# A prepared weight pair that stays on chip, resident loads spread over the steps, and an even credit table for late weight work

## The chip, the core and the metric

One core of a Trainium2 chip runs the whole kernel. The metric is device time in microseconds, as the median of repeated executions; lower is better. The engines are named by short names: PE (TensorE, matrix products), DVE (VectorE), ACT (ScalarE), POOL (GpSimd) and SP (SyncE, which only issues transfers). ACT issues transfers too.

## What is computed

Attention with two softmaxes (queries over the head dimension, keys over the sequence), then two MLPs, all in fp32:

```python
kv  = einsum('bhsd,bhde', softmax(k, seq), v)
x   = softmax(q, head_dim) @ kv          # 8 batches x 576 tokens, 512 wide
h   = x @ w_in1;  g = h * sigmoid(h);           x = g @ w_out1
h   = x @ w_in2;  g = h * clip(h + 3, 0, 6)/6;  out = g @ w_out2
```

There are 4608 tokens, and each MLP goes 512 to 2048 to 512.

## The kernel before

The tokens are cut into 9 blocks of 512 (`NB`), the 2048 hidden columns into 8 pairs of 128-column groups (`NC`); the program calls a pair p. One pair of one block is a cycle g of the first MLP (72 cycles, `PER`) or a step k of the second.

A product with w_in is done on 2 x 2 blocks with seven products instead of eight (Winograd's form), and each fp32 factor is split into a high and a low part, with three matmuls for each product (`mm3`, L76 to L79). So a pair of w_in has to be *prepared*: the raw words are turned into floats, sums of quarters are formed, and seven quarter-size forms are split into high and low. A prepared pair takes 14 KB per partition, 1792 KB in all. `converting` and `operands_w` write this as a list of (cost, function) items: magnitude (ACT), floor, shift, sign, low (DVE), two pairs of sums (DVE), then for two parts of three and four forms a cast on ACT (`high`, L207) and the remainder on DVE (`low`, L211), and a store of each part to DRAM (`keep_part`, L217, issued on ACT).

**First MLP.** `cycle(g)` does the seven w_in products of pair p (into the PSUM banks A, B and C, with the sums L771, L776 and L781 on DVE between them), the gate (`bend`), and between the products the eight w_out products of the cycle before (`layer_out`). The prepared w_in pair for cycle g + 2 is loaded from DRAM into a ring of two tiles (`load_w`). After each group of matmuls comes a `side(k)`, k from 0 to 7. There, from cycle 57 on (`LATE` is 56), the preparation of the second MLP's eight w_in pairs is worked off: `pump(more)` adds `more` to a credit and runs the items whose cost the credit covers. The items of all pairs stand in one list, made by `chain`, which puts the first item of a pair, the load of the next raw weights (`feed`, L101, on ACT) and the last store of the pair before next to one another.

**Second MLP, first half.** `step_in(k, slot)` does the seven products of a step, overlapped with its neighbours. Its prepared pairs stay on chip: pairs 0 and 1 in the ring's two tiles, 2 and 3 in tiles loaded in the last cycle (`keep_in(2, 4, 4)`), 4 to 7 in tiles loaded as the stage begins (`keep_in(4, NC, 6)` loads 4 and 5, the slots of steps 0 and 2 load 6 and 7). Each step's gated values go through one of three `gs` tiles and are stored to DRAM (`gated`, L852, on SP). Beside the steps of a block a pair of w_out is prepared.

**Second half.** `step_out(q)` multiplies the gated values, loaded back as pairs of steps (`load_g`, L939), by the prepared w_out pairs, which `load_out` (through `fill`, L278, on SP) brings into the tiles that the w_in pairs leave: seven loads in the last block's steps 1 to 7 and one behind the last step.

Transfers on SP's queue and on ACT's are issued in the order of the program; an engine that issues a transfer whose operands are not ready waits there.

Of the kernel before, what the change touches and what calls it, by code (L numbers as in the profile page):

```python
# [30 lines left out]
PER = NC * NB  # L31
SCRATCH = 1024


@with_exitstack
def attention_two_mlps(ctx: ExitStack, tc: tile.TileContext, kqT, kv5, qn, w1, w2, out):
# [140 lines left out]
    def operands_w(m, p, new_r, new_s, get_w, add=nc.vector):  # L177

        x = {}

        def sums(k):
            w = get_w()
            if k == 0:
                x["s"] = new_s()
            a22, a11, a12, a21 = (w[:, j * 256:(j + 1) * 256] for j in range(4))
            s1, s2, s3, s4 = (x["s"][:, j * 256:(j + 1) * 256] for j in range(4))
            for o, a, b, op in (
                (s1, a21, a22, ALU.add), (s2, s1, a11, ALU.subtract),
                (s3, a11, a21, ALU.subtract), (s4, a12, s2, ALU.subtract),
            )[2 * k:2 * k + 2]:  # L190
                add.tensor_tensor(out=o, in0=a, in1=b, op=op)

        def parts(k):
            src, n = ((get_w()[:, :768], 3), (x["s"], 4))[k]
            o = slice(0, 3) if k == 0 else slice(3, 7)
            src = src.rearrange("p (s n) -> p s n", n=256)
            if m:
                return x["r", k][:, 0], x["r", k][:, 1], src
            return x["r"][:, 0, o], x["r"][:, 1, o], src

        def high(k):
            if m:
                x["r", k] = m2_p[0].tile([P, 2, 3 + k, 2 * P], F32R, tag=f"r{k if m == 1 else 0}", name="r")
            elif k == 0:
                x["r"] = new_r()
            h, l, src = parts(k)
            nc.scalar.copy(h, src)  # L207

        def low(k):
            h, l, src = parts(k)  # L210
            nc.vector.tensor_tensor(out=l, in0=src, in1=f32(h), op=ALU.subtract)  # L211

        def keep_part(k):
            if (m, p) not in wd:
                wd[m, p] = dram.tile([P, 14 * 256], F32, tag=f"wd{m}{p}", name="wd")
            d = wd[m, p].rearrange("p (h s n) -> p h s n", h=2, n=256)
            nc.scalar.dma_start(out=d[:, :, 3 * k:3 + 4 * k], in_=f32(x["r", k]))  # L217

        def keep():
            wd[m, p] = d = dram.tile([P, 14 * 256], F32, tag=f"wd{m}{p}", name="wd")  # L220
            nc.scalar.dma_start(out=d, in_=f32(x["r"]).rearrange("p h s n -> p (h s n)"))

        if m:
            return [
                (0.85, lambda: sums(0)), (0.85, lambda: sums(1)), (0, lambda: high(0)), (0.95, lambda: low(0)),
                (0, lambda: high(1)), (1.2, lambda: low(1)), (0, lambda: keep_part(0)), (0.5, lambda: keep_part(1)),
            ]
        return [
            (0.85, lambda: sums(0)), (0.85, lambda: sums(1)), (0, lambda: high(0)), (0.95, lambda: low(0)),
            (0.6, lambda: high(1)), (0.6, lambda: low(1)), (0.5, keep),  # L230
        ]
# [20 lines left out]
    def second(p, i, **kw):  # L252
# [8 lines left out]

        return converting(1, p, i, make) + operands_w(1 + i, p, None, s, lambda: x["w"], **kw)

    def chain(jobs):
        out = []
        for k, j in enumerate(jobs):
            out.append(j[0])
            if k:
                out += [(0, feed), jobs[k - 1][-1]]
            out += j[1:-1]  # L270
        return out + [jobs[-1][-1]]

    def load_w(g):
        m, t, p = place(g)
        fill(ring_tile(g), m, p)

# [439 lines left out]
    def cycle(g):  # L716
# [11 lines left out]
        def side(k):  # L728
# [14 lines left out]
            if late and g > LATE and k < 4:  # L743
                pump({NC - 1: (1.2, 0.8, 0.8, 0), 0: (1.2, 1.2, 1.2, 0.7)}.get(p, (2.4, 1.2, 1.2, 0.7))[k], keep=k > 0)
            if p == NC - 2 and k in (6, 7):
# [5 lines left out]
        if g == LATE:  # L751
            attn.close()
            m2_p.append(stack("m2", 1, right, side="right"))
            stream.extend((1, q, 0) for q in range(NC))
            feed(2)
            steps.extend(chain([second(q, 0) for q in range(NC)]))
        if g == PER - 1:
            pump(99)
            right.close()
            keep_in(2, 4, 4)  # L760
        product(g, 1, A[:, lo], True)
# [125 lines left out]
    def beside(k):  # L887
# [16 lines left out]
        def slot(i):  # L904
            if k in (0, 2) and i == 1:
                fill(second_in[6 + k // 2], 1, 6 + k // 2)
            if t < NB - 1:
# [12 lines left out]
    def load_out(p):  # L920
        if p < 2:
            r = ring_tile(2 * PER + p)
# [74 lines left out]
    def last_block(p):  # L997
        if p == 0:
# [4 lines left out]
            load_g(1)  # L1003
        if p:
            load_out(p - 1)

# [146 lines left out]
    with tc.manual_schedule():  # L1153
# [78 lines left out]
        for g in range(NC, PER):  # L1232
            cycle(g)
        second_in[0], second_in[1] = ring[PER], ring[PER + 1]
        for k in range(8):
            layer_out(PER - 1, k)
        weights_1.close()
        load_y(NB + 1)
        keep_in(4, NC, 6)
        sums.close()  # L1240
# [9 lines left out]
        step_in(PER, lambda i: None)  # L1250
        load_out(NC - 1)
        mid.close()
# [4 lines left out]
        out_p["b"] = stack("out_b", 1, mid)  # L1257
        load_g(2)
        load_g(3)
        make_g(2)  # L1260
        make_g(3)
# [56 lines left out]
```

## Time and profile before

| | us |
|---|---|
| median of 3 runs | 1674.35 (1670.68 to 1675.2) |
| the profiled execution | 1680.23 |
| its span | 1678.4 |
| PE busy | 1617.6 (96%) |
| DVE busy | 1194.6 (71%) |
| ACT busy | 767.0 (46%) |
| POOL busy | 249.4 (15%) |

The profile gives for each engine the time in which it was busy, and for stretches of the span also the clock that was granted to PE: 1.00 stands for 2.4 GHz and 0.50 for 1.2 GHz, and a value between them for a mix over the stretch. Matmuls are pipelined, so a matmul's duration (some 280 ns for 256 columns) is longer than the distance to the next one (some 117 ns). Behind an instruction, in brackets, stands how long its engine was idle before it and what ended the idle time.

### The profile page before, as it was taken

How to read it: one execution, taken by the hardware profiler on the slowest of the kernel's cores; microseconds unless marked ns; L12 is line 12 of the kernel's file. 1: busy time of each engine (PE TensorE's matmuls, PEld its weight loads, DVE VectorE, ACT ScalarE, POOL GpSimd, SP SyncE). 2: the span in 40 equal slices, each digit the busy share in tenths (PEclk: the TensorE clock that was granted, in tenths of full speed). 3: DMA queues.
4: the chain of work that ended last, by engine and by line, in shares of the span. 5: the costliest groups of instructions: out<-in, count | busy, mean ns of one | idle time of the engine just before them, and what ended most of it. 6: DMA issues, size and time to landing. Idle time of an engine off the chain costs nothing. (4 is left out here: it accounts for less than half of the span.)

```text
span 1678.4 us, 28093 instructions
## 1 busy us (share of the span) xinstructions
PE 1617.6 (96%) x11112; PEld 1461.3 (87%) x11112; DVE 1194.6 (71%) x1910; ACT 767.0 (46%) x1383; POOL 249.4 (15%) x188
## 2 busy tenths in 40 slices
PE   6999999999999999999999899999999899999998
PEld 4445878888889898988789899999999899999998
DVE  7998686575656647568777577777776587778875
ACT  5544555454444545344444455555554343343332
POOL 2211232222222222200000122222220000000000
PEclk9999999999999999999999999999999899999999
DMA  8589979999899999858888955555558833333332
GB/s 297 188 283 287 241 222 240 264 274 262 211 286 263 246 261 263 232 211 319 298 317 330 367 198 200 195 208 205 201 204 335 331 144 126 127 126 126 126 127 75
DMA packets 90107, 386.62 MB, mean 230 GB/s; under 512 B 21880, under 2 KB 25976, under 8 KB 67960
## 3 DMA queue, kind: packets, MB, share of 16 engines
q1 hardware_dynamic: 77272, 323.49, 61.2%
q10 hardware_dynamic: 12704, 61.35, 10.6%
q8 instruction: 87, 1.43, 0.3%
q14 instruction: 44, 0.36, 0.1%
HBM read 283.90 MB, written 100.90 MB: 229 GB/s over the span
## 5 line engine op out<-in xcount | busy, mean ns | idle before, releaser
L1077 PE MATMUL M<-kout,f 128*128 128x256 f32 x2268 | 273.0, 282 | 2.4 <-DVE f L978 1.9
L1077 PEld LDWEIGHTS M<-kout,f 128*128 128x128 f32 x2268 | 271.4, 190 | 3.2 <-DVE f L978 2.3
L77 PE MATMUL y<-gs,woh 128*128 128x512 f32 x512 | 205.9, 402 | 2.8 <-ACT gs L73 2.8
L78 PE MATMUL y<-gs,woh 128*128 128x512 f32 x512 | 203.4, 397 | 0.2 <-DVE gs L74 0.2
L79 PE MATMUL y<-gs,wol 128*128 128x512 f32 x512 | 201.2, 393 | 0.0
L976 ACT CAST f<-gt 128x1024 fp32r<-128x1024 f32 x72 | 75.6, 1050 | 180.5 <-DVE gt L951 98.9
L77 PE MATMUL B<-o,ring 128*128 128x256 f32 x492 | 142.7, 290 | 14.3 <-DVE s L771 7.6
L74 DVE TENSOR_TENSOR gs<-g,gs 128x512 fp32r<-128x512 f32 x128 | 102.4, 800 | 70.8 <-ACT gs L73 70.0
L79 PE MATMUL B<-o,ring 128*128 128x256 f32 x492 | 139.8, 284 | 0.0
L78 PE MATMUL B<-o,ring 128*128 128x256 f32 x492 | 139.7, 284 | 0.0
L77 PE MATMUL A<-op,ring 128*128 128x256 f32 x444 | 127.2, 286 | 2.2 <-DMA ring<-wd 2.2
L78 PE MATMUL A<-op,ring 128*128 128x256 f32 x444 | 126.0, 284 | 2.4 <-DVE op L578 2.4
L79 PE MATMUL A<-op,ring 128*128 128x256 f32 x444 | 125.8, 283 | 0.0
L619 ACT ACTIVATE g<-A 128x512 f32<-128x512 f32 x72 | 43.0, 598 | 176.3 <-DVE A L776 165.4
L77 PEld LDWEIGHTS B<-o,ring 128*128 128x128 f32 x492 | 93.8, 191 | 31.6 <-DVE s L771 11.8
L79 PEld LDWEIGHTS y<-gs,wol 128*128 128x128 f32 x512 | 97.2, 190 | 21.9
L73 ACT CAST gs<-g 128x512 fp32r<-128x512 f32 x128 | 79.2, 619 | 79.7 <-DVE g L621 78.8
L77 PEld LDWEIGHTS y<-gs,woh 128*128 128x128 f32 x512 | 97.8, 191 | 15.8 <-ACT gs L73 3.0
L978 DVE TENSOR_TENSOR f<-gt,f 128x1024 fp32r<-128x1024 f32 x72 | 88.0, 1222 | 32.2 <-ACT f L976 30.9
L77 PE MATMUL B<-o,kin 128*128 128x256 f32 x324 | 94.5, 292 | 14.5 <-DVE B L862 14.4
L78 PEld LDWEIGHTS y<-gs,woh 128*128 128x128 f32 x512 | 98.0, 192 | 9.4 <-DVE gs L74 0.5
L845 DVE SCALAR_TENSOR_TENSOR g<-a,A 128x512 f32<-128x512 f32 x72 | 49.5, 688 | 75.8 <-ACT a L838 60.8
(224 smaller groups left out, 4219.7 us busy)
## 6 DMA issues: line engine op xcount, KB each, us to landing
ring<-wd SPq DMA_DIRECT2D x66, 1792.0 KB, 10.6
gd<-g SPq DMA_DIRECT2D x72, 512.0 KB, 3.4
gt<-gd SPq DMA_DIRECT2D x36, 1024.0 KB, 4.9
st<-w_dram SPq DMA_DIRECT2D x16, 1024.0 KB, 6.2
st<-w_dram ACTq DMA_DIRECT2D x16, 1024.0 KB, 8.6
wd<-r ACTq DMA_DIRECT2D x16, 1024.0 KB, 5.6
ev<-kv_dram SPq DMA_DIRECT2D x24, 640.0 KB, 9.2
wd<-ring ACTq DMA_DIRECT2D x8, 1792.0 KB, 9.8
```

Of the source, the lines that this page charges most:

```text
L73: nc.scalar.copy(hi, src)
L74: nc.vector.tensor_tensor(out=lo, in0=src, in1=f32(hi), op=ALU.subtract)
L77: nc.tensor.matmul(o, lhsT=wh, rhs=xh, start=start, stop=False, **kw)
L78: nc.tensor.matmul(o, lhsT=wh, rhs=xl, start=False, stop=False, **kw)
L79: nc.tensor.matmul(o, lhsT=wl, rhs=xh, start=False, stop=stop, **kw)
L619: nc.scalar.activation(out=a, in_=hb, func=AF.Tanh, scale=0.5)
L845: nc.vector.scalar_tensor_tensor(out=x["g"][:, j], in0=x["a", j], scalar=1.0, in1=x["AB"[j]], op0=ALU.min, op1=ALU.mult)
L976: nc.scalar.copy(o[0], src)
L978: nc.vector.tensor_tensor(out=o[1], in0=src, in1=f32(o[0]), op=ALU.subtract)
L1077: nc.tensor.matmul(M[:, h * 2 * P:(h + 1) * 2 * P], lhsT=a, rhs=b, start=p == 0 and h == 0 and e == 0, stop=p == NC - 1 and e == 2, skip_g ...
```

## The change

1. The pairs are prepared in the order 0, 2, 3, 4, 5, 6, 7, 1 (`STAYS` is 1). All go through one resident tile, `k1`; pair 1, the last, stays there, is not stored and not loaded again. The ring's second tile gets pair 2, so `keep_in(3, 4, 4)` loads pair 3 alone in the last cycle.
2. `chain` issues the last store of a pair ahead of the load of raw weights.
3. The late credit table is 1.2 for each of four sides in an ordinary cycle, where it was 2.4, 1.2, 1.2 and 0.7, and what is not used is carried over from cycle to cycle.
4. As the second MLP begins, pair 4 is loaded ahead of the read of y, pair 5 behind it, and pairs 6 and 7 in steps 1 and 2.
5. In the last block, w_out pairs 0 to 3 are loaded in steps 1, 3, 5 and 7; pairs 4 to 7 behind the second output step, pair 4 between two loads of gated values.

```diff
         def high(k):
-            if m:
-                x["r", k] = m2_p[0].tile([P, 2, 3 + k, 2 * P], F32R, tag=f"r{k if m == 1 else 0}", name="r")
+            if m == 2:
+                x["r", k] = m2_p[0].tile([P, 2, 3 + k, 2 * P], F32R, tag="r0", name="r")
             elif k == 0:
                 x["r"] = new_r()
...
+            keep_part = store_part if (m, p) != (1, STAYS) else lambda k: None
...
+        def new_r():
+            second_in[p] = kept_p[1].tile([P, 2, 7, 2 * P], F32R, tag="k1", name="kin")
+            return second_in[p]
...
             if k:
-                out += [(0, feed), jobs[k - 1][-1]]
+                out += [jobs[k - 1][-1], (0, feed)]
...
-        fill(ring_tile(g), m, p)
+        fill(ring_tile(g), m, p if g != PER + 1 else 2)
...
-                pump({NC - 1: (1.2, 0.8, 0.8, 0), 0: (1.2, 1.2, 1.2, 0.7)}.get(p, (2.4, 1.2, 1.2, 0.7))[k], keep=k > 0)
+                pump({NC - 1: (1.2, 0.8, 0.8, 0), 0: (1.2, 1.2, 1.2, 0.7)}.get(p, (1.2, 1.2, 1.2, 1.2))[k], keep=True)
...
+            kept_p[1] = stack("kept1", 1, kept, side="right")
...
+            order = [*(q for q in range(NC) if q != STAYS), STAYS]
...
-            keep_in(2, 4, 4)
+            keep_in(3, 4, 4)
...
-            if k in (0, 2) and i == 1:
-                fill(second_in[6 + k // 2], 1, 6 + k // 2)
+            if k in (1, 2) and i == 1:
+                fill(second_in[5 + k], 1, 5 + k)
...
-        if p < 2:
+        if p in (0, 2):
             r = ring_tile(2 * PER + p)
...
-        if p:
-            load_out(p - 1)
+        if p % 2:
+            load_out(p // 2)
...
+        keep_in(4, NC, 5)
         load_y(NB + 1)
-        keep_in(4, NC, 6)
+        fill(second_in[5], 1, 5)
...
-        load_out(NC - 1)
...
         load_g(2)
+        load_out(4)
         load_g(3)
+        for p in range(5, NC):
+            load_out(p)
```

How the order of the work moves stands in three places. The first is ACT in cycles 58 and 59, where the first pair's preparation ends and the second's goes on. `r` are the two tiles of parts, `kin` the resident tile, `wd` the prepared pair in DRAM, `st` the raw weights; the 768-column cast and store are the first part, the 1024-column ones the second. Before:

```order
L207 CAST r<-st 128x1024
L217 DMA wd<-r 256x1x768
L127 ACTIVATE w<-st 128x1024
L101 DMA st<-w_dram 128x2048
L217 DMA wd<-r 256x1x1024
L619 ACTIVATE g<-A 128x512
```

Now:

```order
L208 CAST kin<-st 128x1024
L219 DMA wd<-kin 256x1x768
L128 ACTIVATE w<-st 128x1024
L219 DMA wd<-kin 256x1x1024
L102 DMA st<-w_dram 128x2048
L626 ACTIVATE g<-A 128x512
```

The second store moved ahead of the load of raw weights on ACT's queue.

The second place is SP as the second MLP begins, from the store of the last y block on; `xr` is the read of y, `kin` are resident pairs, `gd` the stores of gated values. Before:

```order
L660 DMA yd_8656<-y 128x2048
L532 DMA xr<-yd_2212 128x2048
L278 DMA kin<-wd 128x3584 x3
L852 DMA gd_8804<-g_8740 128x1024
L852 DMA gd_8804<-g_8801 128x1024
L278 DMA kin<-wd 128x3584
```

Now:

```order
L667 DMA yd_8646<-y 128x2048
L285 DMA kin<-wd 128x3584
L539 DMA xr<-yd_2212 128x2048
L285 DMA kin<-wd 128x3584
L861 DMA gd_8793<-g_8730 128x1024
L285 DMA kin<-wd 128x3584
L861 DMA gd_8793<-g_8790 128x1024
L285 DMA kin<-wd 128x3584
```

One of the three loads ahead of the first store of gated values moved behind it.

The third place is SP from the last steps of that stage to the output steps; `ring` and `kout` are w_out pairs, `gt` loads of gated values. Before:

```order
L278 DMA kout<-wd 128x3584
L852 DMA gd_13289<-g_13221 128x1024
L278 DMA kout<-wd 128x3584
L852 DMA gd_13289<-g_13286 128x1024
L278 DMA kout<-wd 128x3584
L852 DMA gd_13401<-g_13353 128x1024
L278 DMA kout<-wd 128x3584
L852 DMA gd_13401<-g_13398 128x1024
L278 DMA kout<-wd 128x3584
L939 DMA gt<-gd_9072 128x2048
L939 DMA gt<-gd_9208 128x2048
```

Now:

```order
L861 DMA gd_13275<-g_13209 128x1024
L285 DMA ring<-wd 128x3584
L861 DMA gd_13275<-g_13272 128x1024
L861 DMA gd_13385<-g_13339 128x1024
L285 DMA kout<-wd 128x3584
L861 DMA gd_13385<-g_13382 128x1024
L948 DMA gt<-gd_9062 128x2048
L285 DMA kout<-wd 128x3584
L948 DMA gt<-gd_9198 128x2048
L285 DMA kout<-wd 128x3584 x3
L948 DMA gt<-gd_9325 128x2048
```

A w_out load stands behind every second store now, and four of the loads moved behind the first load of gated values for the output steps.

## Rows read from the trace of the kernel before

**Rows 1.** The page: busy time of the engines

```profile
PE 1617.6 (96%) x11112; PEld 1461.3 (87%) x11112; DVE 1194.6 (71%) x1910; ACT 767.0 (46%) x1383; POOL 249.4 (15%) x188
```

**Rows 2.** Stretches, five cycles: length; busy PE, PEld, DVE, ACT, POOL; granted clock, DMA, GB/s

```profile
752.68:764.36 11.68, 10.82 (x68) 9.45 (x66) 9.35 (x16) 5.42 (x10) 0.00 (x0) 1.00 0.70 248
764.36:774.90 10.54, 10.54 (x67) 9.53 (x66) 8.13 (x12) 5.35 (x9) 0.00 (x0) 1.00 0.96 333
796.15:811.03 14.88, 12.44 (x67) 10.76 (x67) 8.62 (x15) 5.98 (x10) 0.00 (x0) 0.89 0.76 269
821.58:834.35 12.77, 11.08 (x67) 9.36 (x66) 10.55 (x18) 6.44 (x13) 0.00 (x0) 1.00 0.88 305
865.99:881.66 15.67, 12.62 (x67) 10.81 (x66) 9.54 (x14) 6.59 (x11) 0.00 (x0) 0.89 0.84 295
```

**Rows 3.** Timeline of PE: start, duration, instruction, idle time before it

```profile
655.70 0.39 PE L77 MATMUL B<-o,ring 128*128 128x256 f32 x1 [1.56 <-DVE s L771]
...
806.58 0.38 PE L77 MATMUL B<-o,ring 128*128 128x256 f32 x1 [2.44 <-DVE B L781]
...
870.41 0.50 PE L77 MATMUL y<-gs,woh 128*128 128x512 f32 x1 [2.83 <-ACT gs L73]
...
959.16 0.58 PE L77 MATMUL B<-o,kin 128*128 128x256 f32 x1 [6.25 <-DVE B L862]
...
1306.15 0.58 PE L77 MATMUL B<-o,kin 128*128 128x256 f32 x1 [3.66 <-DVE B L862]
...
1331.73 0.39 PE L1077 MATMUL M<-kout,f 128*128 128x256 f32 x1 [1.01 <-DVE f L978]
```

**Rows 4.** Table by stretches behind four waits of PE (columns as in rows 2)

```profile
957.30:964.00 6.70, 4.84 (x22) 4.85 (x23) 4.64 (x10) 2.92 (x6) 0.27 (x1) 0.50 0.59 243
1305.50:1312.20 6.70, 6.05 (x28) 6.05 (x29) 3.96 (x7) 0.69 (x1) 0.00 (x0) 0.50 1.00 422
1332.80:1336.10 3.30, 3.30 (x17) 3.30 (x17) 3.23 (x5) 0.34 (x2) 0.00 (x0) 0.50 0.46 107
655.00:664.00 9.00, 8.30 (x50) 7.49 (x51) 7.56 (x14) 5.52 (x12) 3.42 (x2) 1.00 1.04 281
```

**Rows 5.** Timeline of ACT: second stores, casts that waited, one gate

```profile
787.09 0.52 ACTq L217 DMA_DIRECT2D wd<-r  x1
...
802.95 1.05 ACT L207 CAST r<-st 128x1024 fp32r<-128x1024 f32 x1 [3.94 <-DMA wd<-r]
...
850.64 1.22 ACTq L217 DMA_DIRECT2D wd<-r  x1
...
868.80 1.04 ACT L207 CAST r<-st 128x1024 fp32r<-128x1024 f32 x1 [6.33 <-DMA wd<-r]
...
1301.72 0.69 ACT L838 ACTIVATE a<-A,half 128x512 f32<-128x512 f32 x1 [3.02 <-DVE A L870]
```

**Rows 6.** Timeline of DVE: three waits for transfers

```profile
956.87 0.69 DVE L845 SCALAR_TENSOR_TENSOR g<-a,A 128x512 f32<-128x512 f32 x1 [7.39 <-DMA gd<-g]
...
1304.46 0.69 DVE L845 SCALAR_TENSOR_TENSOR g<-a,A 128x512 f32<-128x512 f32 x1 [2.84 <-DMA gd<-g]
...
1327.67 0.69 DVE L951 TENSOR_TENSOR tg<-gt 128x512 f32<-128x512 f32 x1 [6.02 <-DMA gt<-gd]
```

**Rows 7.** Timeline of SP as the second MLP begins: issues, from first to last

```profile
930.99 2.58 SPq L278 DMA_DIRECT2D kin<-wd  x3
941.35 5.20 SPq L852 DMA_DIRECT2D gd<-g  x2
```

**Rows 8.** Lines L217 (stores), then L101 (raw weight loads), 755 to 930 us

```profile
DMA to landing us min/median/max: 4.1/6.4/13.9
...
DMA to landing us min/median/max: 6.5/9.8/11.8
```

**Rows 9.** Table by stretches with loads queued up; last column GB/s

```profile
915.00:930.00 15.00, 15.00 (x84) 13.09 (x83) 11.33 (x19) 7.38 (x14) 0.00 (x0) 1.00 1.00 427
945.00:959.00 14.00, 7.90 (x68) 7.70 (x66) 6.13 (x11) 3.75 (x8) 7.89 (x8) 0.94 1.01 420
```

More of the change, by code (lines that the diff above doesn't have):

```diff
@@ L32 @@
 SCRATCH = 1024
+STAYS = 1
 @with_exitstack
@@ L201, in high @@
         def high(k):
-            if m:
-                x["r", k] = m2_p[0].tile([P, 2, 3 + k, 2 * P], F32R, tag=f"r{k if m == 1 else 0}", name="r")
+            if m == 2:
+                x["r", k] = m2_p[0].tile([P, 2, 3 + k, 2 * P], F32R, tag="r0", name="r")
             elif k == 0:
@@ L211, in low, with store_part @@
             nc.vector.tensor_tensor(out=l, in0=src, in1=f32(h), op=ALU.subtract)
-        def keep_part(k):
+        def store_part(k):
             if (m, p) not in wd:
@@ L216, in keep_part @@
             d = wd[m, p].rearrange("p (h s n) -> p h s n", h=2, n=256)
-            nc.scalar.dma_start(out=d[:, :, 3 * k:3 + 4 * k], in_=f32(x["r", k]))
+            o = slice(3 * k, 3 + 4 * k)
+            nc.scalar.dma_start(out=d[:, :, o], in_=f32(x["r", k] if m == 2 else x["r"][:, :, o]))
         def keep():
@@ L260, in s @@
             return words[1, p, i].rearrange("p n w -> p (n w)")[:, :2 * DM].bitcast(F32)
-        return converting(1, p, i, make) + operands_w(1 + i, p, None, s, lambda: x["w"], **kw)
+        def new_r():
+            second_in[p] = kept_p[1].tile([P, 2, 7, 2 * P], F32R, tag="k1", name="kin")
+            return second_in[p]
+        return converting(1, p, i, make) + operands_w(1 + i, p, new_r, s, lambda: x["w"], **kw)
     def chain(jobs):
@@ L752, in cycle @@
             attn.close()
+            kept_p[1] = stack("kept1", 1, kept, side="right")
             m2_p.append(stack("m2", 1, right, side="right"))
-            stream.extend((1, q, 0) for q in range(NC))
+            order = [*(q for q in range(NC) if q != STAYS), STAYS]
+            stream.extend((1, q, 0) for q in order)
             feed(2)
-            steps.extend(chain([second(q, 0) for q in range(NC)]))
+            steps.extend(chain([second(q, 0) for q in order]))
         if g == PER - 1:
@@ L1233, in attention_two_mlps @@
             cycle(g)
-        second_in[0], second_in[1] = ring[PER], ring[PER + 1]
+        second_in[0], second_in[2] = ring[PER], ring[PER + 1]
         for k in range(8):
```

## The prediction

> **What bounds the kernel now.** I read the page first: TensorE (PE) is busy for 96% of the span [rows 1], so only time in which PE stands still, or runs at the lower clock, can be won. I then read PE's own timeline for its waits, then the table by stretches for the granted clock, then the waits of ScalarE (ACT), VectorE (DVE) and SyncE (SP) that end PE's waits. Behind the last cycle with attention work there are four places; the change touches all of them and nothing before them.
>
> *Late cycles, 57 to 71.* A cycle that is not disturbed takes 10.54 us, at full clock [rows 2]. Four of the fifteen are longer: 11.68, 14.88, 12.77 and 15.67 us, which is 12.8 us over 4 x 10.54. In the second and fourth PE waits 2.44 and 2.83 us [rows 3], and the mean granted clock is 0.89: some 3.3 us of each stand at 0.50, the 1.2 GHz level, and lose half of that, 1.7. Both begin on ACT: the cast of the four-sum part has to wait 3.94 and 6.33 us for the previous pair's store of that part, which was issued 15.9 and 18.2 us earlier behind a 1 MB weight load on the same queue [rows 5].
>
> *Start of the second MLP.* PE waits 6.25 us [rows 3] and then works 4.84 us at 0.50 [rows 4], a loss of 2.4: 8.65 us. DVE had waited 7.39 us for a store of gated values [rows 6], issued 941.35 behind three resident loads, issued together from 930.99 [rows 7].
>
> *End of that stage.* PE waits 3.66 us [rows 3] and works 6.05 us at 0.50 [rows 4], a loss of 3.0: 6.7 us. The reader sees the same cause: DVE waits 2.84 us for a store of gated values [rows 6], while eight w_out loads are issued one a step.
>
> *First output steps.* PE waits 1.01 us, then 3.3 us at 0.50 [rows 3, 4]: 2.7 us. DVE had waited 6.02 us for a load of gated values [rows 6] that stood behind the w_out loads.
>
> Together 12.8 + 8.65 + 6.7 + 2.7 = 30.85 us.
>
> **The change part by part.**
>
> *Prepared pairs go through one resident tile.* One store and one load of 1.8 MB fall away. Nobody on PE waits for either of them today, so by themselves I cost them at 0; the transfers beside them are the cover. The two tiles of parts become one tile, so the first cast of the next pair now waits for both stores of the pair before. That wait is new and no row shows it. From the second store's issue to that cast lie, by the table of credits and by where ACT reaches each side of a cycle, 8.7 to 11.4 us. The store now stands in front of the weight load. Bounds: it lands as the weight loads did that stood there, in 6.5 to 11.8 us, or as stores do at their latest, 13.9 us [rows 8]. So the wait is between nothing and 5.2 us. I take nothing, since the store's new place is that of the load and the middle one of those landed in 9.8 us; a wait of 3 us at the sides where most of these casts now stand is covered, because the next cast on ACT has some 3 us to spare there.
>
> *The weight load moves behind the store.* ACT issues the same three DMAs per pair. The load then takes the second store's place, which landed in 15.9 and 18.2 us where ACT waited for it [rows 5], and stores where their landing is on record in 6.4 in the middle [rows 8]. It is used 13.2 us after its issue (pair 4), 14.2 (pair 6) or 14.9 to 20.8. I take the middle of 6.4 and 18.2, some 12 us: no wait; the upper end is 5 us at two places.
>
> *Even credits.* 4.8 a cycle carried over, instead of 2.4 at the first side with the rest dropped. The same operations run, 0 us in sum. The 1.1 us of cycle 57 goes, since half of its DVE work moves behind the sum that PE waits for. In cycles 61 and 70 a cast and its remainder now stand ahead of that sum: some 0.65 us each. Cycle 63 keeps 0.5 to 1.2 of its 2.2 us. With 0.5 for what I do not see, 3.0 us stay of 12.8: **9.8 gained**.
>
> *Resident loads of the second MLP.* In front of the first gated store there are now two loads and not three; one load before the stage is gone as well, but the queue runs dry then. A load is 1.835 MB, and the stretches with loads queued up moved 427 and 420 GB/s [rows 9], so 4.3 us a load. The store lands some 4.8 us earlier, near 952.0, DVE waits 2.5 instead of 7.4 us, and PE had 1.14 us (7.39 less 6.25) to spare: 1.4 us stay. The next two stores each have a load in front: 2.36 MB, 5.5 us, against steps of 4.95, so some 0.8 us each. Sum 3.0 of 8.65: **5.65 gained**. Moved past on SP: the read of y behind pair 4 lands some 4 us later, about when ACT first wants it (945.4); pairs 6 and 7 are then in place 2 us before their steps. The Trainium skill (DMA: Bandwidth & Descriptors, Specifications) gives about 358 GB/s as what HBM yields to one core; by that the 6.8 MB ahead of the store would take 3.3 us more and the sum would end at 1654.6. The rows show 420 and more.
>
> *w_out loads.* Four are issued on every second step, four after the second output step, interleaved with loads of gated values. A store of gated values in the last steps then has at most one load in front. DVE's 2.84 us goes, yet PE still waits there: ACT's gate ends at 1302.41 [rows 5] and from DVE's use of it to PE's restart are 1.7 us (1304.46 to 1306.15) [rows 3, 6], so PE, ready at 1302.4, would wait 1.8. Does that drop the clock? 1.56 us did not (the window behind it at 1.00), 2.44 did [rows 3, 4]. 1.8 is nearer to the former, so no: 6.7 less 1.8, **4.9 gained**; with a drop 3.2. For the output steps the load of gated values is now first in an empty queue: **2.7 gained**. The four late loads need, from the eighth us after the first output matmul, 4.3 us each with two 1 MB loads between, and land 1 to 3 us before their steps of 4.97 us. Little room, but I cost them at 0.
>
> Sum: 9.8 + 5.65 + 4.9 + 2.7 = 23.05. The profiled execution took 1680.23 (span 1678.4); it would take 1657.2. The median of the timed runs is 5.9 lower, 1674.35; I subtract from that: **1651.3**.
>
> **The rivals.**
>
> *1. The weight load is late.* Nothing else is disturbed, but at one or two places ACT waits up to 4 us for it, PE 3, and 1.7 of half clock follow: 4.7 to 9.4, so 1656 to 1661. For it: the two stores of [rows 5], whose place it takes. Against: the stretches are more even now.
>
> *2. The late w_out loads miss their steps.* Each of the last three 2.5 us late, plus half clock twice (3.4): 10.9, so 1662. For it: such a load takes 10.6 us to land in the middle of all ring loads. Against: [rows 9].
>
> *3. One tile is too few: slower.* If each second store needs 14 us or more from its issue, as the two in [rows 5] did, every one of the seven pairs that follow a store pays what the two waits cost today, 4.3 and 5.1, mean 4.7: 33 us in place of 12.8. The other places give 13.25, so 1674.35 + 20.2 - 13.25 = 1681. It decides at about 12 us from issue to landing. Against: these stores stood behind a load that now stands behind them. The Trainium skill (Trainium Kernel Development and Optimization, Best Practices) asks for double buffers so that DMA and compute overlap; that speaks for this rival, and the two waits of [rows 5], with a buffer for each part, agree in kind.
>
> *4. The gains are given back.* The change does what it says, but stays on PE move elsewhere by some 20 us: 1670 to 1675.
>
> **How the numbers follow.** Forecast 0.50, with its own bounds 1643.5 (all 30.85 us) and 1656; rival 1 0.22; rival 2 0.10; rival 3 0.06; rival 4 0.08; a gain of which I misplace the parts 0.04. A difference of 0.3% is 5 us, about what a measurement of this kernel can tell. Faster by more than that (under 1669.3): 0.87; within: 0.08; slower: 0.05. The range takes in the forecast and the first two rivals, 1642 to 1665, with 1.5 us below the sum of what is lost for places I do not see.
>
> **What would show it.** Right: in the late cycles the casts into the resident tile wait under 1 us for stores, and no cycle but 61, 63 and 70 is over 11 us; the first DVE wait for gated stores is 2 to 3 us; DVE's wait at the first output steps is gone; half clock at no place behind cycle 57. Wrong: ACT waits of 3 us or more for stores or weight loads, PE waits on w_out loads in output steps 4 to 7, or a time above 1665.

## The result, and the profile after

| | before | after |
|---|---|---|
| median of the timed runs, us | 1674.61 (4 runs, 1670.68 to 1675.2) | 1653.6 (4 runs, 1650.19 to 1654.42) |
| profiled execution, us (span) | 1680.23 (1678.4) | 1654.42 (1652.6) |

The ratio is 0.9876, with a 95% interval of 0.9855 to 0.9896. It is 21.0 us less; the prediction was 1651.3, the changed kernel is 2.3 us slower than that. One execution of the later run 2 fell into a slower state (1744.05 us, granted clock 0.851) and is left out of that run's median.

The first line of the page answers to [rows 1]: PE is busy for 10 us less (a matmul at half clock, the 1.2 GHz level, takes longer, and fewer of the same 11112 now run at it) and idles 16 us less.

```profile
PE 1607.8 (97%) x11112; PEld 1450.8 (88%) x11112; DVE 1191.6 (72%) x1910; ACT 766.7 (46%) x1383; POOL 251.6 (15%) x188
```

To see where the time went I cut both traces at the same matmuls: the first of cycle 57, the first of the second MLP, the first output product, and the first of output step 6. First the table by stretches of the kernel before, then that of the changed kernel (columns: stretch, its length, busy time of PE, of the weight loads, DVE, ACT, POOL, then the granted clock, DMA share and GB/s).

```profile
0.00:752.68 752.68, 721.34 (x4050) 588.71 (x4051) 522.02 (x882) 363.25 (x729) 180.07 (x124) 0.99 0.90 251
752.68:929.32 176.64, 168.60 (x1016) 149.51 (x1014) 129.83 (x213) 78.17 (x133) 0.00 (x0) 0.98 0.85 321
929.32:1307.59 378.27, 363.77 (x3025) 360.20 (x3024) 265.55 (x472) 193.05 (x372) 69.34 (x64) 0.99 0.64 235
1307.59:1343.23 35.64, 34.12 (x254) 33.62 (x253) 22.84 (x28) 11.77 (x14) 0.00 (x0) 0.89 0.77 313
1343.23:1678.41 335.18, 329.79 (x2774) 329.25 (x2772) 254.38 (x317) 120.75 (x137) 0.00 (x0) 1.00 0.35 122
```

```profile
0.00:747.44 747.44, 719.53 (x4051) 585.95 (x4052) 519.74 (x882) 363.44 (x729) 181.46 (x124) 1.00 0.90 253
747.44:916.18 168.74, 165.75 (x1015) 146.64 (x1014) 128.76 (x213) 78.14 (x133) 0.00 (x0) 1.00 0.83 317
916.18:1286.20 370.02, 361.28 (x3025) 357.72 (x3024) 266.04 (x472) 192.68 (x372) 70.09 (x64) 1.00 0.64 229
1286.20:1317.48 31.28, 31.28 (x253) 31.28 (x253) 21.02 (x25) 11.51 (x13) 0.00 (x0) 0.95 1.01 391
1317.48:1652.60 335.12, 329.98 (x2774) 329.19 (x2772) 256.08 (x319) 120.92 (x137) 0.00 (x0) 1.00 0.36 129
```

The late cycles are 7.9 us shorter, the second MLP's first half 8.25, the first six output steps 4.4, the rest as long as before: 20.5 together, close to the 21.0 of the medians. The first stretch is 5.2 us shorter as well, but the program is the same there, so this belongs to the two executions and not to the change.

**Late cycles**, answering to [rows 2]: the two cycles of 15 us are gone, and no stretch is at a lower clock. Five cycles are longer than 10.7 us; four of them:

```profile
747.44:759.11 11.67, 11.08 (x68) 9.37 (x66) 9.35 (x16) 5.29 (x10) 0.00 (x0) 1.00 0.70 249
...
769.66:780.95 11.29, 10.81 (x68) 9.45 (x66) 8.11 (x14) 5.54 (x9) 0.00 (x0) 1.00 0.75 304
812.59:824.12 11.53, 10.82 (x67) 9.47 (x67) 9.01 (x15) 6.37 (x11) 0.00 (x0) 1.00 0.69 272
824.12:835.91 11.79, 11.08 (x68) 9.34 (x66) 11.72 (x21) 5.74 (x12) 0.00 (x0) 1.00 0.82 297
```

They are cycles 57, 59, 63 and 64; cycle 66 has 11.48. ACT's timeline answers to [rows 5]: the casts into the resident tile (L208) wait for no store. These are the second store of a pair (issued by ACT's queue, L219) and the next pair's first cast, one pair as an example: they are 10.6 us apart, and what the cast waits 0.46 us for is DVE.

```profile
798.26 0.52 ACTq L219 DMA_DIRECT2D wd<-kin  x1
...
808.90 0.83 ACT L208 CAST kin<-w 128x768 fp32r<-128x768 f32 x1 [0.46 <-DVE w L146]
```

**Second MLP.** On SP's queue two resident loads (`kin`) now stand ahead of the first store of gated values (`gd`), then one, where [rows 7] had three:

```profile
917.38 0.42 SPq L285 DMA_DIRECT2D kin<-wd  x1
...
918.77 0.73 SPq L285 DMA_DIRECT2D kin<-wd  x1
928.15 0.32 SPq L861 DMA_DIRECT2D gd<-g  x1
928.57 0.39 SPq L285 DMA_DIRECT2D kin<-wd  x1
```

DVE's waits for these stores answer to [rows 6]: 2.37 us where it was 7.39, then 1.23 and 2.10.

```profile
938.67 0.69 DVE L854 SCALAR_TENSOR_TENSOR g<-a,A 128x512 f32<-128x512 f32 x1 [2.37 <-DMA gd<-g]
...
944.18 0.69 DVE L854 SCALAR_TENSOR_TENSOR g<-a,A 128x512 f32<-128x512 f32 x1 [1.23 <-DMA gd<-g]
...
949.70 0.69 DVE L854 SCALAR_TENSOR_TENSOR g<-a,A 128x512 f32<-128x512 f32 x1 [2.10 <-DMA gd<-g]
```

PE's waits of over 1 us behind cycle 57 answer to [rows 3], and the windows behind the first and the last of them to [rows 4]:

```profile
941.32 0.39 PE L78 MATMUL B<-o,kin 128*128 128x256 f32 x1 [1.59 <-DVE B L871]
...
1262.08 0.39 PE L78 MATMUL B<-o,ring 128*128 128x256 f32 x1 [1.46 <-DVE B L871]
...
1285.19 0.38 PE L78 MATMUL B<-o,kin 128*128 128x256 f32 x1 [1.93 <-DVE B L871]
```

```profile
941.40:948.20 6.80, 6.80 (x58) 6.80 (x59) 4.97 (x9) 3.85 (x7) 3.57 (x3) 1.00 1.00 418
...
1285.70:1289.10 3.40, 3.40 (x18) 3.40 (x18) 1.86 (x3) 0.69 (x1) 0.00 (x0) 0.51 1.09 337
```

Only the last wait is followed by the 1.2 GHz level, for 3.4 us: 1.7 us lost, and most of that falls into the first output step. The wait of 1.01 us in the output steps is gone, and so is one of 0.51 us just ahead of it. DVE still waits 7.10 us for a load of gated values, but at 1322, behind the sixth output step, and PE does not wait for it.

### The profile page after: what moved, and what is told of

It is laid out like the page before. It is cut to its first block, busy times and chain, and to the rows that moved or that the text cites. A ratio compares the mean times of both kernels' runs of the same rounds, so it can differ in the third digit from the quotient of the medians.

```text
span 1652.6 us, 28084 instructions
## 1 busy us (share of the span) xinstructions
PE 1607.8 (97%) x11112; PEld 1450.8 (88%) x11112; DVE 1191.6 (72%) x1910; ACT 766.7 (46%) x1383; POOL 251.6 (15%) x188
## 4 chain that ended last, share of the span: by engine, by line
PE 67%; DVE 16%; DMA 9%; ACT 4%; issue 3%; POOL 0%; ACTq 0%; SPq 0%; DVEq 0%; POOLq 0%
PE M L1086 20%; PE y L78 5%; PE y L79 5%; PE y L80 5%; PE B L78 4%; PE B L79 4%; PE B L80 4%; PE A L78 4%; PE A L80 4%; PE A L79 4%; DMA ring<-wd 3%; DMA gd<-g 2%; DMA gt<-gd 1%; PE C L80 1%; PE C L79 1%
```

## Experiments

The theory to begin with was the prediction's, mended at one point: the order of store and load took the two long waits away; what stays in the late cycles is DVE work that stands where it stands because credit of the first MLP is carried into cycle 57; the second MLP gains from the transfers that no longer stand in front of gated values. The rivals were that even credits alone do it, that the single tile costs what the order gives, and that one load fewer does what the spreading is credited with. In the table a stage is measured between the same first matmuls as above (the last column to the last matmul); each median stands beside runs of the kernel before on the same chip, and the ratio is to those.

| kernel | median, us | ratio (95%) | late cycles | 2nd MLP, first half | output |
|---|---|---|---|---|---|
| before | | | 176.6 | 378.3 | 366.0 |
| after | 1653.6 | 0.9876 (0.9855 to 0.9896) | 168.75 | 370.0 | 361.85 |
| 1 credit from zero | 1653.17 | 0.9878 (0.9854 to 0.9903) | 166.1 | 369.4 | 361.3 |
| 2 load ahead of store | 1664.56 | 0.9946 (0.992 to 0.9971) | 179.3 | 369.3 | 361.7 |
| 3 old credits | 1651.7 | 0.9874 (0.985 to 0.9897) | 165.85 | 368.3 | 361.7 |
| 4 old resident loads | 1657.9 | 0.9907 (0.9882 to 0.9931) | 168.2 | 374.2 | 361.8 |
| 5 old w_out loads | 1662.13 | 0.9915 (0.9886 to 0.9945) | 168.4 | 371.6 | 366.0 |
| 6 before, store first | 1662.88 | 0.993 (0.9903 to 0.9957) | 165.9 | 377.1 | 365.0 |
| 7 end of stage | 1652.19 | 0.9853 (0.9824 to 0.9882) | 168.6 | 367.2 | 360.5 |
| 8 credit from zero and end | 1646.66 | 0.9826 (0.9796 to 0.9855) | 166.3 | 366.8 | 361.7 |
| 9 old credits and end | 1651.95 | 0.9835 (0.9809 to 0.9861) | 165.9 | 366.25 | 360.8 |
| 10 before, even credits | 1673.37 | 0.9966 (0.9945 to 0.9988) | 169.2 | 376.0 | 367.1 |
| 11 after again | 1654.05 | 0.9879 (0.986 to 0.9897) | 168.2 | 370.2 | 361.8 |
| 12 as 8, beside 11 | 1651.15 | 0.9862 (0.9839 to 0.9885) | 165.7 | 367.1 | 362.2 |

The interval of a ratio reaches 3.4 to 4.9 us to either side. The late cycles repeat within 0.6 us: after and runs 4, 5, 7 and 11 have the same program there and take 168.2 to 168.75. The second MLP's first half repeats less well: 368.3 to 370.2 in after and runs 1, 2, 3 and 11, which are the same there. So differences of 2 or 3 us are read from the stages, and in the second MLP from the waits as well.

### 1. Credit from zero

```diff
-            steps.extend(chain([second(q, 0) for q in order]))
+            steps.extend(chain([second(q, 0) for q in order])); credit[0] = 0.0
```

> The changed kernel with the credit set to zero at cycle 56, so that the 2.6 us of credit left by the first MLP's own preparation are not spent at the first side of cycle 57. Theory (the prediction's table of credits was right but began at zero, and the carried credit is what kept cycle 57 long): cycle 57 falls from 11.67 to some 10.6 us, every later item moves 2.6 us of credit later, the long cycles 59, 64 and 66 become short and 61, 63 and 70 cost some 0.6 each; the late stage falls from 168.75 by 1 to 2 us, the time from 1653.6 to about 1652. Rival (the stays of the late cycles come from elsewhere, such as stores and loads, and not from where DVE's items stand): cycle 57 stays over 11.3 us and the time stays within 1 us of the changed kernel's.

Cycles 57, 61 and 70 of this run:

```profile
748.48:759.03 10.55, 10.55 (x68) 9.53 (x67) 8.24 (x14) 4.33 (x8) 0.00 (x0) 1.00 0.81 274
790.67:801.96 11.29, 10.81 (x68) 9.45 (x67) 8.11 (x14) 5.54 (x9) 0.00 (x0) 1.00 0.77 311
887.29:898.56 11.27, 10.79 (x67) 9.44 (x66) 8.32 (x14) 4.50 (x8) 0.00 (x0) 1.00 0.46 170
```

Cycle 57 is clean, and 61 and 70 are 0.74 and 0.72 longer, where the prediction had 0.65 each; 64 and 68 cost 0.5 and 0.4, which it did not name, 63 costs nothing, and 2.4 us stay in all, where it had 3.0. So its table of credits was wrong above all in its first number. What the carried credit does is plain in DVE's timeline of cycle 57, first of the changed kernel, then of this one: with 2.6 us to spend (the most that `pump` lets a credit grow to), three conversions (L131, L134, L140) run ahead of the sum that PE waits for (L780), against one.

```profile
750.55 0.69 DVE L131 TENSOR_SCALAR w<-w 128x1024 f32<-128x1024 f32 x1 [1.62 <-ACT w L128]
751.28 0.69 DVE L134 TENSOR_SCALAR w<-w 128x1024 uint32<-128x1024 uint32 x1
752.01 1.23 DVE L140 SCALAR_TENSOR_TENSOR w<-st,w 128x1024 uint32<-128x1024 uint32 x1
753.15 0.42 DVE L780 TENSOR_TENSOR s<-B,s 128x256 f32<-128x256 f32 x1
```

```profile
751.59 0.69 DVE L131 TENSOR_SCALAR w<-w 128x1024 f32<-128x1024 f32 x1 [1.63 <-ACT w L128]
752.21 0.42 DVE L780 TENSOR_TENSOR s<-B,s 128x256 f32<-128x256 f32 x1
```

The stage falls by 2.7 us, more than expected; the median does not show it. On ACT the room is smaller here: two casts wait for a store, 0.71 and 1.33 us, and ACT waits 2.64 us for staged weights at 864, just ahead of cycle 68. In run 8, which has the same credits, the weights wait is 2.83 us and cycle 68 costs 0.6; in run 12, the same kernel, it is 0.52 us and cycle 68 costs nothing.

### 2. The load ahead of the store, as before

```diff
-                out += [jobs[k - 1][-1], (0, feed)]
+                out += [(0, feed), jobs[k - 1][-1]]
```

> The changed kernel with the old order in ACT's queue alone: the weight load of the pair after next ahead of the second store, all else as changed (one resident tile, even credits). Theory (the order is what took ACT's waits for stores away: a store behind a 1 MB load needs 14 to 18 us to land): ACT's casts into the resident tile wait 2 to 6 us for the store at several pairs, since all pairs now share one tile; PE waits 2 to 3 us with half clock behind it at 3 to 7 places; the late stage gains 8 to 25 us on the changed kernel's 168.75, the time is 1662 to 1678. Rival (the even credits leave enough time between store and cast, whatever the order): no ACT wait for a store over 1 us, late stage within 1 us, time 1653 to 1655.

Expected, and found: ACT's timeline has the second store behind the weight load (L102), and the next pair's first cast waits for it.

```profile
799.74 0.33 ACTq L102 DMA_DIRECT2D st<-w_dram  x1
800.10 1.24 ACTq L219 DMA_DIRECT2D wd<-kin  x1
...
814.42 0.83 ACT L208 CAST kin<-w 128x768 fp32r<-128x768 f32 x1 [5.05 <-DMA wd<-kin]
...
847.56 1.47 ACTq L219 DMA_DIRECT2D wd<-kin  x1
...
864.34 0.83 ACT L208 CAST kin<-w 128x768 fp32r<-128x768 f32 x1 [7.23 <-DMA wd<-kin]
```

From issue to release are 14.3 and 16.8 us. Five casts wait 19.2 us together; PE waits 2.41 us behind the longest, with 3.4 us of half clock after it. The late cycles gain 10.5 us and are longer than before the change: this is rival 3 in kind, and what it decides by is where the load stands. Its price is half of the forecast one: 15.6 us stay in the late cycles, where rival 3 had 33, since not every pair waited and only one wait brought half clock.

### 3. The old credits

```diff
-{...}.get(p, (1.2, 1.2, 1.2, 1.2))[k], keep=True)
+{...}.get(p, (2.4, 1.2, 1.2, 0.7))[k], keep=k > 0)
```

> The changed kernel with the old table of credits (2.4 at a cycle's first side, what is left of it before that dropped). Theory (even credits are worth the two or three stays on DVE in cycles 57, 61 and others, not the stores): the carried credit is dropped at cycle 57, which still costs 1.1 us by the two DVE steps at its first side; stays of 1 to 2 us as in cycle 61 before come at two or three cycles; late stage 169 to 173, time 1654 to 1658. Rival a (the credits also set the distance from store to cast and with one tile the wait for the store comes back): ACT waits of over 2 us for stores, time over 1660. Rival b (the credits do nothing): within 1 us of 1653.6, with cycles as long as in the changed kernel.

Both the theory and its rivals fall. The late cycles are 2.9 us *shorter* than in the changed kernel: 1.1 us stay in cycle 57 and 1.1 in 63, nothing else. One cast waits 2.5 us for a store, and PE does not notice. With store first and one tile the even credits as changed, with credit carried in, cost 2.9 us and bring nothing.

### 6 and 10. The order alone, and the credits alone, on the kernel before

```diff
@@ 6: before
-                out += [(0, feed), jobs[k - 1][-1]]
+                out += [jobs[k - 1][-1], (0, feed)]
@@ 10: before
-{...}.get(p, (2.4, 1.2, 1.2, 0.7))[k], keep=k > 0)
+{...}.get(p, (1.2, 1.2, 1.2, 1.2))[k], keep=True)
```

> The kernel before with one thing changed: in ACT's queue the second store of a pair stands ahead of the weight load, not behind it; two tiles for the parts, the old credits, and all eight pairs stored and loaded as before. Theory (the order alone took away the two long waits in the late cycles, and the even credits gave nothing): no ACT wait for a store over 2.5 us, the late stage falls from 176.6 to 165.5 to 168, the time from 1672.5 (the median of the runs of before beside this study) to 1661 to 1665; the waits at the start of the second MLP and at its end stay as they were. Rival a (one tile and no store of the last pair are needed too, since 1.8 MB less is moved): late stage 170 to 175. Rival b (the weight load, now second, lands late): ACT waits over 2 us for the staged weights and the time is 1668 or more.

> The kernel before with the even credits alone: 1.2 at each of four sides, carried over; old order in ACT's queue, two tiles for the parts, all pairs stored and loaded, old resident and w_out loads. Theory (the order of store and load is what costs; even credits do not take the waits away): ACT still waits 2 to 6 us for a store at two or more casts, half clock stands behind at least one of them, the late stage stays between 173 and 182 against 176.6, the time is 1670 to 1680. Rival (even credits spread the transfers so that the waits go as well): no wait for a store over 2 us, late stage 166 to 170, time 1664 to 1668.

The order alone takes 10.7 of the 12.9 us that the late cycles lost, with two tiles and every pair stored: no cast waits for a store, and rival a falls. In the late cycles its stores (L217) land in 3.9 to 9.5 us, where [rows 8] had 4.1 to 13.9, with 6.4 in the middle both times. ACT waits 2.97 us for staged weights once, at 922, behind the late cycles. The stores of the whole run:

```profile
DMA to landing us min/median/max: 3.9/5.5/10.1
```

The credits alone did not do what I expected. ACT still waits for stores, as the theory said:

```profile
800.59 1.05 ACT L207 CAST r<-st 128x1024 fp32r<-128x1024 f32 x1 [3.33 <-DMA wd<-r]
...
881.30 1.05 ACT L207 CAST r<-st 128x1024 fp32r<-128x1024 f32 x1 [2.50 <-DMA wd<-r]
```

But these waits are shorter than those of [rows 5], PE waits less than 1 us behind them, the clock holds, and the late cycles are 7.4 us shorter; the theory's 173 to 182 was wrong. The 169.2 lies in the rival's range, though not for its reason, as the waits did not go. So there are two cures for one wait, and they do not add: order 10.7, credits 7.4, both with one tile 7.9. (As the second MLP starts, PE waits 3.83 us for a ring load in this run, with 3.4 us at half clock behind it, but then 1.55 us behind DVE's store of gated values where it was 6.25. The stage is 2.3 us shorter than before, so nothing of the 7.4 is lost there.)

### 4. The old resident loads

```diff
-        keep_in(4, NC, 5)
         load_y(NB + 1)
-        fill(second_in[5], 1, 5)
+        keep_in(4, NC, 6)
...
-            if k in (1, 2) and i == 1:
-                fill(second_in[5 + k], 1, 5 + k)
+            if k in (0, 2) and i == 1:
+                fill(second_in[6 + k // 2], 1, 6 + k // 2)
```

> The changed kernel with the resident loads of the second MLP issued as before: y, then pairs 4 and 5 before the stage, pair 6 at step 0 and pair 7 at step 2. Theory (loads in front of the first store of gated values made DVE wait): DVE's first wait for gated values is 6 to 8 us instead of 2 to 3, PE waits 5 to 6 us with half clock behind it, and the first half of the second MLP gains 5 to 7 us on the changed kernel's: time 1658.5 to 1661. Rival (one load fewer, that of the pair that stays on chip, is what helped, and the spreading nothing): within 1.5 us of 1653.6.

DVE's first wait for gated values, then PE's wait behind it, and the window after that:

```profile
939.50 0.69 DVE L854 SCALAR_TENSOR_TENSOR g<-a,A 128x512 f32<-128x512 f32 x1 [6.66 <-DMA gd<-g]
```

```profile
941.87 0.58 PE L78 MATMUL B<-o,kin 128*128 128x256 f32 x1 [5.58 <-DVE B L871]
```

```profile
941.90:945.30 3.40, 3.40 (x17) 3.40 (x18) 1.86 (x4) 1.16 (x3) 0.00 (x0) 0.55 0.81 319
```

Both waits came back; the stage gains 4.2 us, less than the 5 to 7 expected, since the clock fell for 3.4 us and not for 6.8, and PE's second wait there, 0.51 us at 952 in the changed kernel, fell away. The median, 1657.9, is a little under the 1658.5 expected. The one load fewer is worth little: DVE waits 6.66 us with it and 7.39 before. The spreading is what helped; the rival (one load fewer does it) falls.

### 5. The old w_out loads

```diff
-        if p % 2:
-            load_out(p // 2)
+        if p:
+            load_out(p - 1)
...
         step_in(PER, lambda i: None)
+        load_out(NC - 1)
...
-        load_out(4)
         load_g(3)
-        for p in range(5, NC):
-            load_out(p)
```

> The changed kernel with the w_out loads as before: one a step in the last block, pair 7 behind the stage, none later. Theory (a w_out load a step stood in front of the stores of gated values and of the loads of gated values for the output): DVE waits 2 us or more for a store of gated values in the last two steps and 5 us or more for the load of gated values at output step 2 or 3; PE waits 3 us or more at the end of the stage and 1 us in the output steps, each with half clock behind it. Against the changed kernel, whose end of stage still loses 1.9 us to a wait and 1.7 to half clock, the second MLP gains 2 to 4 us and the output steps 3 to 5: time 1658 to 1662. Rival (the loads of gated values for the output land late whatever the w_out loads do): output steps as long as in the changed kernel, time within 2 us of 1653.6.

PE's wait at the end of the stage and in output step 4, and DVE's wait for the load of gated values:

```profile
1289.14 0.58 PE L78 MATMUL B<-o,kin 128*128 128x256 f32 x1 [3.00 <-DVE B L871]
...
1314.97 1.45 PE L1086 MATMUL M<-kout,f 128*128 128x256 f32 x7 [1.01 <-DVE f L987]
```

```profile
1310.91 0.69 DVE L960 TENSOR_TENSOR tg<-gt 128x512 f32<-128x512 f32 x1 [6.27 <-DMA gt<-gd]
```

Half clock stands behind both. The first half of the second MLP gains only 1.6 us, as the wait that the changed kernel has at 1262 is 0.73 here instead of 1.46; the output gains 4.2. By the stages the part is worth 5.8 us, with some 2 us of doubt from the second MLP's own scatter.

### 7. The end of the stage

```diff
         nc.vector.tensor_tensor(out=w["B"][:, hi], in0=w["B"][:, lo], in1=w["s5"], op=ALU.add)
+        if k == PER:
+            gated(k - 1, 0)
+            gated(k - 2, 1)
         if x:
...
-        if x:
+        if x and k < PER - 1:
             gated(k, 0)
-        if k:
+        if 0 < k != PER - 1:
             gated(k - 1, 1)
...
-            4: s(0), 5: s(1), 6: s(2), 7: s(3) + f(0, 0, 0), 8: f(0, 0, 1) + f(0, 1, 0), 9: f(0, 1, 1),
+            5: s(0), 6: s(1), 7: s(2), 8: s(3) + f(0, 0, 0), 9: f(0, 0, 1) + f(0, 1, 0), 10: f(0, 1, 1),
...
```

> The changed kernel with two edits at the end of the second MLP: in its last step the two gate products on DVE stand behind the sum that PE waits for, not ahead of it, and the differences of gated values for the output start half a step later on DVE. Theory (PE's last wait of 1.6 to 1.9 us is DVE's order, as the prediction's 1.8 says, and the wait near 1262 us is the load of gated values that DVE meets half a step too early): both waits fall under 0.5 us and no half clock stands at the end of the stage; the second MLP falls from 370.0 by 2.5 to 4.5 us, the time to 1649 to 1651. Rival (what PE waits for comes later anyway: ACT's gates, or the bank that the first output matmul needs): the wait reappears at the next matmuls or at the first output step, and the time stays within 1 us of 1653.6.

PE's last wait is 0.53 us, that at 1262 is gone, the clock holds, and the stage is 2.9 us shorter than after (over 1 us shorter than run 3, the shortest without the edits), the output 1.4 (half clock had spilled into it). The median, 1652.19, is over the 1649 to 1651 expected. The rival falls by the trace: nothing waits in their place.

```profile
1281.40 0.39 PE L78 MATMUL B<-o,kin 128*128 128x256 f32 x1 [0.53 <-DVE B L871]
```

### 8, 9, 11 and 12. The edits together, and the changed kernel again

Run 8 is run 1 and run 7 together, run 9 is run 3 and run 7 together; 11 and 12 are the changed kernel and the kernel of run 8 once more, side by side on one chip.

> The changed kernel with the credit set to zero at cycle 56 and the two edits at the end of the second MLP together. Theory (the two are independent): late stage 166.1 as with the reset alone, second MLP 366 to 368, time 1647 to 1649.5, ahead of both kernels. Rival (the gains do not add, since the profile's differences of 2 to 3 us are given back elsewhere): the time is 1651 or more.

> The changed kernel with the old table of credits and the two edits at the end of the second MLP. Theory (with the store ahead of the load, the old credits leave 2.2 us of stays in the late cycles, against 2.4 with even credits from zero and 5.0 as changed): late stage 165.5 to 166.2, second MLP 366 to 368, time 1646 to 1649, the same as the version with the credit reset within 2 us. Rival (the single cast that waits 2.5 us for a store under the old credits becomes longer in other runs and costs PE): late stage over 168, time over 1650.

> The changed kernel as it is, beside the next run, so that the two are compared on one chip. Theory: 0.986 to 0.989 of the kernel before, as in the first comparison (0.9876), late stage 168.5 to 169, second MLP 369.5 to 370.5. Its end of stage shows whether a PE wait of 1.6 to 1.95 us there brings half clock: with a wait over 1.9 it does, under 1.7 it does not. Rival: the clock falls or holds there whatever the wait's length.

> The version with the credit reset and both edits at the end of the second MLP, run again beside the changed kernel. Theory: 5 to 7 us faster than the changed kernel of the same call (2.4 in the late cycles, 3.2 at the end of the second MLP), so 0.982 to 0.985 of the kernel before. Rival: the earlier difference was that of two chips, and the two are within 3 us.

By the stages the edits add: the late cycles and the second MLP together are 533.1 and 532.8 us in runs 8 and 12, 532.2 in run 9, against 538.8 and 538.4 in the changed kernel and run 11. That is 5.6 to 6.6 us. In runs 8 and 12 the output is no shorter than after (361.7 and 362.2), so run 7's gain there is not found again. The medians agree in sign only: 0.9826 and 0.9862 against 0.9876 and 0.9879, and 2.9 us on the shared chip, under the 5 to 7 expected and inside the 3 us of the rival; five executions of each, 1647.99 to 1654.42 and 1651.14 to 1655.18, overlap. So that the version is faster as a whole is not shown beyond the stages. Run 9's median, 1651.95, missed its 1646 to 1649. In the profiled pair run 12 came to cycle 57 1.5 us later than run 11, in a stretch that the edits do not touch. Both credit tables do equally well once the store is first (runs 8 and 9).

Run 11 repeats PE's last wait of the stage with 1.92 us and the fall of the clock behind it; run 1 has 1.62 us there and no fall. Runs 2, 3 and 4 have 1.62 to 1.63 as well and none of them falls. First run 11, then run 1:

```profile
1285.49 0.38 PE L78 MATMUL B<-o,kin 128*128 128x256 f32 x1 [1.92 <-DVE B L871]
```

```profile
1285.90:1289.30 3.40, 3.40 (x18) 3.40 (x18) 1.61 (x3) 0.69 (x1) 0.00 (x0) 0.50 1.09 331
```

```profile
1283.11 0.38 PE L78 MATMUL B<-o,kin 128*128 128x256 f32 x1 [1.62 <-DVE B L871]
```

```profile
1283.40:1286.80 3.40, 3.40 (x31) 3.40 (x31) 1.89 (x3) 0.69 (x1) 0.00 (x0) 1.00 1.09 330
```

## Why the prediction was right, and where it was off

**The sum.** 23.05 us were forecast and 20.5 found in the stages: the late cycles gave 7.9 and not 9.8, the second MLP with the first output steps 12.6 and not 13.25. That last pair is closer than its parts: the second MLP gave 8.25 where 10.55 were forecast, the first output steps 4.4 where 2.7 were, partly because half clock runs over the cut between them. Of the signs named as right three came: casts that wait for no store, a first DVE wait of 2.37 us, and no wait of DVE for a load in the first output steps. Two did not: cycles 57, 59, 64 and 66 are over 11 us, where only 61, 63 and 70 were to be, and half clock stands for 3.4 us at 1285.7.

**Casts into one tile: nothing.** Right, and for the reason given: the store took the load's place. In the changed kernel from a second store to the next cast lie 10.1 to 11.4 us (16.9 at one pair; 8.7 to 11.4 forecast), and the stores landed within that. The prediction's spare 3 us were there too: in run 3 a cast waited 2.5 us and its cycle stayed at 10.55. Rival 3 was priced by the two stores of [rows 5], which stood behind a load; run 2 puts them there again and 10.5 us of its price come due. What spoke for it was a rule of the Trainium skill (Trainium Kernel Development and Optimization, Best Practices), double buffers. By the runs, with the store behind the load a second buffer is worth some 10 us (169.2 in run 10 with two tiles, 179.3 in run 2 with one, even credits in both); with the store first it is worth nothing to PE (165.9 in run 6 with two tiles and no cast that waits, 165.85 in run 3 with one tile and one cast that waits, old credits in both). These pairs of runs also differ in the order of the pairs and in one store, so the tile by itself is not isolated.

**The weight load behind the store: no wait.** Right. In the changed kernel ACT waits for staged weights once, 1.2 us at 923, behind the late cycles, and PE does not wait for it. Rival 1 did not come. It came nearest with the credit from zero, 2.64 us in run 1 and 2.83 in run 8, so there is little room.

**Even credits: this step failed.** The prediction said that cycle 57's 1.1 us goes and that 61 and 70 pay 0.65 each. It began the table of credits at zero. The change carries credit over, and so the 2.6 us left by the first MLP's own preparation too: three conversions run at the first side of cycle 57, which stays at 11.67, and all later work stands earlier than the table had it, so that 59, 63, 64 and 66 pay. With the credit set to zero 2.4 us stay, where the forecast had 3.0 (run 1). A second thing the prediction did not see, because it costed the parts of the change together: the even credits were not needed. Store first leaves 2.2 us with the old ones, and 5.0 as changed (runs 3 and 6).

**Resident loads.** 5.65 us forecast. DVE's wait is 2.37 us (2.5 forecast), PE's first wait 1.59 (1.4), and the clock holds. Counted by PE's waits 2.1 us stay (1.59 and 0.51) where 3.0 were forecast. The estimate by the Trainium skill's 358 GB/s (DMA: Bandwidth & Descriptors, Specifications) put the store 3.3 us later; worked out again, 6.8 MB at that rate take 3.1 us more than at 427. The stretch from 928 to 940, with that store and these loads in it, moved 429 GB/s, and the store came when the forecast's 420 and more said. That the total lies nearer to the 1654.6 of that rule is not its doing.

**End of the stage.** 4.9 us forecast, with 1.8 of wait and no fall of the clock. In the profiled execution the wait was 1.93, and the clock fell for 3.4 us: 3.1 us gained, the forecast's other bound, 3.2. In runs 1 to 4 the wait was 1.62 or 1.63 and the clock held: some 5.0 gained. So both of the forecast's cases occur, and which of them a run meets was not foreseen. The wait at 1262, where DVE waits 3.16 us for a load of gated values, was not named in the prediction: 0.76 us before, 1.46 now. The runs do not show it to be the change's: with the old w_out loads it is 0.73 (runs 5 and 10) to 1.49 us (run 6), with the new ones 0.95 to 1.46 (after and runs 1 to 4 and 11).

**Output steps.** 2.7 us forecast; PE's wait and the half clock of its own went, as said. The stretch is 4.4 us shorter since a wait of 0.51 us went as well and since half clock from the end of the stage spilled into it before for 4.6 us and now for 2.9, which costs 0.85 us less; some 0.3 us stay unexplained. The late w_out loads missed no step in the changed kernel, so rival 2 did not come; in run 12 one of them kept PE 0.35 us, so there is no room to spare.

**Rival 4** (given back later) is out: the rest after the sixth output step is 335.1 and 335.2 us.

## What to carry to other kernels

Where a store frees the buffer of the next piece and a load as large goes out on the same queue, issue the store first, and only then think of more buffers or of pacing: here the order alone took 10.7 of 12.9 us, and the pacing on top, with its budget carried in, cost 2.9 (from zero next to nothing: 166.1 against 165.85). When a budget is carried over from one stretch of a program to another, write down what it holds at the border. Undo each part of a change that came as one, since two of its parts may cure the same wait.

## What was not expected

- Up to cycle 57 all fourteen profiled executions run the same program, yet cycle 57 starts between 744.5 us (run 4) and 752.7 (before). In the records the 1.2 GHz level stands there for 3.4 to 17.0 us in all, at places from 25 to 244 us. With such a scatter medians of five runs do not tell 3 us apart here. The clock explains only a part of it: run 12 has the 17.0 us and starts cycle 57 at 749.8, the kernel before has 10.2 us and starts it last.
- A store of 0.8 or 1 MB needed 3.9 to 9.5 us in the late cycles of run 6, where the second of a pair was issued ahead of a 1 MB load, and 11.6 to 16.8 from issue to the waiting cast in run 2, where five casts waited for one behind the load; the load had 8.2 to 12.9 in the late cycles of run 6. Which of the two is late is chosen by the order, and PE waited only when it was the store.
- After a PE wait of 1.92 or 1.93 us the clock fell twice out of twice, after 1.62 or 1.63 at the same place in four runs not once. Why the wait is of one or the other length stays open. Nor does a wait's length alone decide: in output step 4 the clock fell behind waits of 0.51 and 1.01 us in the kernel before ([rows 3, 4]), of 0.70 and 1.01 in run 5, and held behind a longer one, 1.73 us, and the 1.01 that follows it, in run 6. Its first wait, and the window from behind the second:

```profile
1313.86 0.50 PE L1077 MATMUL M<-kout,f 128*128 128x256 f32 x2 [1.73 <-ACT f L976]
```

```profile
1315.40:1318.80 3.40, 3.40 (x27) 3.30 (x28) 3.39 (x4) 1.33 (x2) 0.00 (x0) 1.00 0.30 43
```

Not tried: the pair that stays on chip alone, two tiles with store first and even credits, and an earlier issue of the late w_out loads.
